# Attention and a feed-forward block in one kernel: strips of 64 key rows, two head pairs in one product

## The chip, the cores and the metric

The program runs on one core of a Trainium2 chip. Its time is the device time of one execution in microseconds (us). The core has five engines that run their own instruction streams and wait for each other by semaphores: TensorE (PE) for matrix products, VectorE (DVE), ScalarE (ACT), GpSimd (POOL) and SyncE (SP). Here POOL and SP do hardly any arithmetic: they issue DMA transfers. PE reads its operands from SBUF, an on-chip memory of 128 partitions, and writes into PSUM, which this kernel treats as eight banks of 128 partitions by 512 float32 columns.

## The reference

There are two stages. The first is attention with 4 batches, 8 heads, 768 positions and a head dimension of 64, where a query sees the 96 positions up to its own and the first 8 positions of the sequence (the global keys):

```python
scores = scale * np.matmul(q, k.transpose(0, 1, 3, 2))
rel = pos[:, None] - pos[None, :]
is_global = pos[None, :] < 8
is_local = (rel >= 0) & (rel < 96)
keep = is_global | is_local
dist = np.where(is_global & ~is_local, 96.0, np.abs(rel))
slopes = 2.0 ** (-(np.arange(8) + 1))
scores = scores - slopes[:, None, None] * dist
scores = np.where(keep, scores, -1e9)
a = np.exp(scores - scores.max(-1)); a = a / a.sum(-1)
x = np.matmul(a, v)
```

The eight heads side by side make 3,072 tokens of 512 numbers. The second stage is a gated feed-forward block (FFN) of width 1,536 over them:

```python
g = x @ w_gate
out = (g * (1 / (1 + np.exp(-g))) * (x @ w_val)) @ w_out
```

The output is float32, 3,072 by 512.

## The kernel before

**What sets the order.** The text `ORDER` (L39 to L118) lists some 1,500 steps, and the loop at its end (L726) runs them one after the other. Each step is a name with numbers, and each engine executes its own instructions in the order in which the steps stand. No scheduler moves anything. A step of DMA loads is issued by the engine that its function names: POOL for most loads (which convert float32 to float16 on the way), SP for the first ones, for transposing transfers and for the outputs, ACT for two early loads. A load that stands behind a step with a wait on the same engine waits too.

**Attention.** The 768 keys are cut into seven chunks of 120 rows (`KC`), and every chunk has the 8 global keys in front of it, so that a chunk fills the 128 partitions. Chunk c can only be seen by the 216 queries (`WIN`) from position 120c on. A step of scores (`c`, L471) multiplies the keys of some chunks with the queries that see them, for one pair of heads, into two PSUM banks. Batch 0 does this in four units per head pair (two of each half of 384 queries) with 128 key rows in a product; there a bias product (`B`, L461) first puts minus slope times distance into the banks, from `slopeI` (the identity times the slope) and `dist` (the table of distances). Batches 1 to 3 do it in two units per pair, with the chunk's lower and upper 64 rows in separate 64x64 products that leave out the queries that the 64 rows cannot see. `x` (L531) takes the exponential from PSUM into a buffer `at` in float16, up to three activations per unit, since the lower and upper rows cover different columns. Where no bias was added, `m` (L554) multiplies `at` with `masks`, the exponential of minus slope times distance, which ACT makes by `M` (L333) in two parts for each head.

**Sums and values.** `w` (L582) is issued three times per batch, group g of four heads and half: once with columns of ones for the sums of each query's weights, and twice with V, each time the even or the odd ones of its 64 columns, in four 32-wide tiles side by side. `i` (L612) turns the sums with a 32x32 block transpose and inverts them, `r` (L619) spreads the inverse back over the columns, `p` (L631) multiplies values by it and writes `xT`, the input of the FFN; `n` (L606) first copies the values out of PSUM, where the banks are wanted. One token block (a half of 384 queries of one batch) needs four such products, one for each pair of heads.

**FFN.** For each of 8 token blocks t and 12 column blocks f, `g` and `v` (L642) make gate and value products of 4 steps of 128x128 by 384 columns; the very first ones are cut in two (`ga` and `gb`), so that they can begin with half of `xT`. `t` (L653) takes a tanh on ACT, `s` (L657) and `h` (L664) finish the hidden block on DVE, `o` (L684) multiplies by w_out and `e` (L693) scales and stores. Weights come in slabs of 256 KB (`Lw`, L309), each needed before the first product that reads it.

**The start.** Batch 0 needs q and k turned by PE (`T`, L360: 6 transposes for one head pair, one half of the sequence, q or k). Its loads are 192 KB each: `Lf` on SP or ACT in float32 with a `cast` behind, `Lh` on POOL. Copies `k` and `q` (L368, L392) then bring the turned rows into `kT` and `qT`. `fill` (L339) is a run of products of ones that computes nothing. Batch 1 is turned by PE too (`U`), batches 2 and 3 by transposing transfers (`D`, L425). V comes in chunks of 120 rows (`Lv`, L264), `G` copies the 8 global rows in front of each chunk and `Z` clears the rows that no key has.

**PSUM.** `double` (L225) deals two neighbouring banks to scores and values, `single` (L235) one bank to everything else; a step that gets a bank waits on the chip until the bank's last reader is done.

## Time and profile before

Three runs took 237.44, 237.06 and 235.99 us; the median is 237.06. One further execution was recorded by the profiler; its own time is its span, 234.3 us from the first to the last instruction that the profile shows.

| Engine | busy, us | share of the span | instructions |
|---|---|---|---|
| PE (products) | 228.1 | 97% | 2,520 |
| PEld (weight loads, beside PE) | 132.0 | 56% | 2,520 |
| DVE | 171.5 | 73% | 422 |
| ACT | 134.6 | 57% | 240 |
| POOL | 77.3 | 33% | 103 |

The 16 DMA engines moved 25.5 MB in 88,196 packets; 68% of their time in the span went to the POOL queue's packets and 20% to those of SP and ACT. The mean rate over the span was 109 GB/s, and near 200 in the first third. The granted clock of PE is 9 tenths or more in all 40 slices of the page.

How to read the lines: a row names the line of the code, the engine, the operation, its output and inputs by the program's names (`banks` is PSUM), its shape in partitions by elements, the type, and a count. Groups give busy time and the mean of one in ns, then the time that the engine was idle just before, with what ended most of that idle time. The chain of waits gives start and length of each step in us.

### The profile page before, as it was taken

To read this page: it belongs to the slowest core of one execution; us is meant where nothing else is said; L and a number is where in the kernel's file an instruction comes from. 1 tells how busy PE (TensorE), PEld (TensorE's weight loads), DVE (VectorE), ACT (ScalarE), POOL (GpSimd) and SP (SyncE) were. 2 spreads that over 40 slices of the span, in tenths; PEclk is the share of its full clock that TensorE was granted. 3 is DMA by queue.
4 is the path that set the end of the run, shared out by engine and by line. 5 is a ranking of instruction groups with operands and counts; after the bars stand their busy time and mean duration, and the time that the engine had idled before them with its cause. 6 is when DMAs were issued, how large, how long until landed. Compare 5 with 4: busy or idle time off the path is not lost.

```text
span 234.3 us, 6170 instructions
## 1 busy us (share of the span) xinstructions
PE 228.1 (97%) x2520; PEld 132.0 (56%) x2520; DVE 171.5 (73%) x422; ACT 134.6 (57%) x240; POOL 77.3 (33%) x103
## 2 busy tenths in 40 slices
PE   6999999999999999999999999999999999999994
PEld 4466566555546655655555655555666556555442
DVE  3899998867888798889785788678858794835200
ACT  3899654797883624989834489963554143312031
POOL 8976485461999666880000000000000000000000
PEclk9999999999999999999999999999999999999999
DMA  6999999999999999999042261001110001000224
GB/s 177 173 182 205 197 194 200 192 156 201 141 134 186 158 183 158 181 158 151 3 134 60 83 111 45 22 26 45 48 48 0 4 0 45 4 0 0 90 109 159
DMA packets 88196, 25.54 MB, mean 109 GB/s; under 512 B 78016, under 2 KB 85224, under 8 KB 88168
## 3 DMA queue, kind: packets, MB, share of 16 engines
q0 software_dynamic: 66992, 13.77, 68.3%
q1 hardware_dynamic: 20488, 10.80, 20.4%
q10 hardware_dynamic: 688, 0.59, 0.7%
q8 instruction: 19, 0.31, 0.6%
q14 instruction: 9, 0.07, 0.1%
HBM read 28.51 MB, written 6.29 MB: 149 GB/s over the span
## 4 chain that ended last, share of the span: by engine, by line
PE 90%; DMA 4%; POOL 2%; DVE 1%; ACT 1%; issue 0%; DVEq 0%; POOLq 0%
PE banks L649 54%; PE banks L690 25%; PE banks L596 6%; PE banks L491 3%; DMA k<-in_k_dram 3%; DMA kN<-kst 1%; PE banks L679 1%; POOL vS L282 1%; POOL q L262 1%; PE banks L402 1%; PE banks L364 0%; POOL vS L267 0%; ACT kT L377 0%; POOL k L262 0%; DVE dT L615 0%
## 5 line engine op out<-in xcount | busy, mean ns | idle before, releaser
L655 ACT ACTIVATE th<-banks 128x384 f32<-128x384 f32 x96 | 44.5, 493 | 57.1 <-PE banks L649 55.7
L649 PE MATMUL banks<-xT,wv 128*128 128x384 f16 x384 | 73.5, 326 | 0.0
L649 PE MATMUL banks<-xT,wg 128*128 128x384 f16 x384 | 72.1, 326 | 0.0
L665 DVE TENSOR_TENSOR hT<-banks,sl 128x384 f16<-128x384 f32 x96 | 51.2, 550 | 23.2 <-PE banks L649 22.0
L690 PE MATMUL banks<-wo,hT 128*128 128x512 f16 x276 | 67.8, 379 | 0.0
L539 ACT ACTIVATE at<-banks 64x960 f16<-64x960 f32 (+6 forms) x76 | 58.7, 804 | 3.7 <-PE banks L491 2.5
L659 DVE SCALAR_TENSOR_TENSOR sl<-th,banks 128x384 f32<-128x384 f32 x96 | 50.7, 545 | 12.5 <-ACT th L655 11.9
L649 PEld LDWEIGHTS <-wv 128*128 128x128 f16 x384 | 36.6, 98 | 27.8 <-issue 0.3
L649 PEld LDWEIGHTS <-wg 128*128 128x128 f16 x384 | 36.9, 98 | 25.9
L690 PEld LDWEIGHTS <-hT 128*128 128x128 f16 x276 | 26.7, 98 | 27.1
L564 DVE TENSOR_TENSOR at<-at,masks 128x864 f16<-128x864 f16 (+5 forms) x62 | 25.5, 459 | 3.9 <-ACT at L539 3.9
L267 POOL DMA_DIRECT2D vS<-in_v_dram x28 | 25.4, 912 | 6.8 <-DMA qT<-qst 1.8
L708 ACT ACTIVATE osb<-banks 128x512 f32<-128x512 f32 x23 | 13.5, 597 | 24.2 <-PE banks L690 18.9
L305 POOL DMA_DIRECT2D kst<-in_k_dram x20 | 16.9, 846 | 11.4 <-PE banks L690 6.6
L305 POOL DMA_DIRECT2D qst<-in_q_dram x20 | 17.0, 860 | 3.6 <-DMA wo<-in_moe_w_out_dram 3.2
L491 PE MATMUL banks<-qT,kT 64*64 64x160 f16 (+9 forms) x408 | 12.3, 226 | 0.0
L596 PE MATMUL banks<-at,vS 128*32 128x216 f16 (+6 forms) x576 | 11.7, 225 | 0.1
L608 ACT COPY ns<-banks 128x768 f32<-128x768 f32 x10 | 7.9, 800 | 5.9 <-PE banks L596 5.9
L615 DVE STREAM_TRANSPOSE dT<-banks 128x384 f32<-128x384 f32 x16 | 9.2, 576 | 2.8 <-PE banks L596 2.5
L596 PEld LDWEIGHTS <-vS 128*32 128x32 f16 x576 | 9.8, 95 | 2.1 <-issue 1.9
L491 PEld LDWEIGHTS <-kT 64*64 64x64 f16 (+1 forms) x408 | 7.6, 104 | 5.6 <-issue 4.3
L632 DVE TENSOR_TENSOR xT<-ns,rb 128x384 f16<-128x384 f32 x20 | 10.5, 543 | 0.0
(57 smaller groups left out, 115.7 us busy)
## 6 DMA issues: line engine op xcount, KB each, us to landing
out_dram<-osb SPq DMA_DIRECT2D x23, 256.0 KB, 2.1
vS<-in_v_dram POOLq DMA_DIRECT2D x24, 120.0 KB, 7.0
qst<-in_q_dram POOLq DMA_DIRECT2D x20, 96.0 KB, 6.7
kst<-in_k_dram POOLq DMA_DIRECT2D x20, 96.0 KB, 6.1
wg<-in_moe_w_gate_dram POOLq DMA_DIRECT2D x6, 256.0 KB, 8.2
wv<-in_moe_w_val_dram POOLq DMA_DIRECT2D x6, 256.0 KB, 8.8
wo<-in_moe_w_out_dram POOLq DMA_DIRECT2D x3, 512.0 KB, 12.2
k<-in_k_dram POOLq DMA_DIRECT2D x3, 192.0 KB, 6.2
```

Of the source, the lines that this page charges most:

```text
L267: nc.gpsimd.dma_start(out=v_of(b)[r0:r0 + n, c, :, :], in_=v[b, :, KC * c:KC * c + n, :].rearrange("h p d -> p h d"))
L305: nc.gpsimd.dma_start(out=rows_of(i, b, h // 2)[:, :, h % 2, :], in_=KQ[i][b, h].rearrange("(t p) d -> p t d", p=128))
L491: nc.tensor.matmul(sc[k0:k1, hi, col:col + n], lhsT=keys[r, k0:k1], rhs=qTs[b, hp][r, q0:q0 + n], start=fresh, stop=True, skip_group_check ...
L539: nc.scalar.activation(out=out, in_=src, func=AF.Exp, scale=scale)
L564: ENG[e].tensor_mul(a2, a2, m[:, :, m0:m0 + n])
L596: nc.tensor.matmul(dst[r, o:o + n], lhsT=vSs[b][:, c, 4 * g + j, what - 1::2] if what else ones[:, 0:32], rhs=ats[b, hp, side(b, u)][:, j ...
L649: nc.tensor.matmul(gv[t, f, which][:, 0:TB], lhsT=w[:, c, 128 * f:128 * f + 128], rhs=xTs[t][:, c, :], start=(c == 0), stop=(c == NC - 1))
L655: nc.scalar.activation(out=th, in_=gv[t, f, 0][:, 0:TB], func=AF.Tanh, scale=0.5)
L659: nc.vector.scalar_tensor_tensor(out=sl, in0=gv[t, f, "t"], scalar=1.0, in1=gv[t, f, 0][:, 0:TB], op0=AluOp.add, op1=AluOp.mult)
L665: nc.vector.tensor_mul(hTs[t][:, f, :], gv[t, f, 1][:, 0:TB], gv[t, f, "s"])
L690: nc.tensor.matmul(ops_t[t, i], lhsT=hTs[t][:, f, 128 * i:128 * i + 128], rhs=wo[:, f, :], start=(f == 0), stop=(f == NFF - 1))
L708: nc.scalar.mul(out=osb, in_=ops, mul=0.5)
```

## The change

**Scores.** The 128 rows of a chunk are cut into a lower and an upper 64 rows for all batches, and a unit is now one strip: for one batch, one group g of four heads, one half of the queries, and lower or upper rows (`up`). Its 128 partitions hold the 64 rows for one head pair of the group and the same 64 rows for the other. Table `PIECES` says which chunk, which columns and which queries belong to a strip; strips are 480, 400, 488 and 504 columns wide for each of two heads. There are 32 strips in all, and each takes one exponential over all its columns and, in batches 1 to 3, one product with a mask. A buffer `at` is one of a rotating pool of eleven.

**Masks, distances.** The distance table has 64 rows for strips, held twice: the second copy is divided by 4, since the slope of the second pair of a group is a quarter of the first's. So four masks and four slopes serve eight heads, and a mask covers one half at a time (992 or 880 columns). The table comes in two loads.

**Values and sums.** A strip's rows for one pair stand on partitions 0 to 63 and for the other pair on 64 to 127, so the values use 64x64 tiles, four of them at once. Half of these tiles need V on the other 64 partitions than the one it was loaded to; `cross` (step `X`) copies those parts within SBUF by four SP transfers into `vX`. There are five such steps: two in batch 0, one in each later batch. The sums (`w`) are one step for all eight heads of a batch and half, with `pick` (ones in 16 columns for each pair) as the weights; `i` inverts them once for each batch and half, with two reciprocals and four copies of 32 rows; `r` spreads once for each of four `xT` rows.

**The rest.** The slabs of w_gate and w_val give each partition two rows of 1 KB at a distance of 128 rows instead of two neighbouring ones; V has two buffers instead of three; the clearing of corners of `at` (`zc`) is gone. `ORDER` is a new text with the new steps.

```diff
+PIECES = [
+    [[(1, 0, 120, 152), (0, 152, 0, 160), (2, 312, 240, 144), (3, 456, 360, 24)],
+     [(1, 0, 176, 160), (0, 160, 64, 152), (2, 312, 296, 88)]],
+    [[(3, 0, 384, 128), (4, 128, 480, 152), (5, 280, 600, 152), (6, 432, 720, 48),
+      (2, 480, 384, 8)],
+     [(3, 0, 416, 160), (4, 160, 536, 160), (5, 320, 656, 112), (2, 432, 384, 72)]],
+]
+WIDTH = [[480, 400], [488, 504]]
+COL0 = [[0, 480], [880, 1368]]
+COLS = 1872
...
+    return np.concatenate([d, d / 4]).astype(np.float16)
...
-Lf.S.0.1 zc.1.V Z.0.P pre Lf.A.1.1 cast.0.1.V Lf.A.1.0 Li sl.3 Ld.S Z.3.P fill.14 sl.7 sl.0 T.1.0.0
...
+Li pre Lh.0.0.4.8 Ld.S.1 fill.14 T.2.0.0 Lf.S.0.1 Lh.0.1.0.4 Z.0.P fill.2 Lh.1.0.4.8 Ld.S.0 sl.2
...
+    def cross(b, c0, c1):
+
+        if b not in crossed:
+            crossed[b] = sb2.tile([128, NCH, NP, D], FP16, name="vX", tag="vX")
+        for r in range(2):
+            to, of = slice(64 * r, 64 * r + 64), slice(64 - 64 * r, 128 - 64 * r)
+            for g in range(2):
+                h = 4 * g + 2 * r
+                nc.sync.dma_start(
+                    out=crossed[b][to, c0:c1, 2 * g:2 * g + 2], in_=vSs[b][of, c0:c1, h:h + 2])
...
-            in_=src[256 * g:256 * g + 256, f0:f0 + WF].rearrange("(p s) f -> p s f", s=2))
+            in_=src[256 * g:256 * g + 256, f0:f0 + WF].rearrange("(s p) f -> p s f", s=2))
...
+    def make_masks(i, half):
         nc.scalar.activation(
-            out=masks[:, h, c0:c1], in_=dist[:, c0:c1], func=AF.Exp, scale=-slopes[h])
-        made.add((h, part))
+            out=masks[:, i, columns(half)], in_=dist[:, columns(half)], func=AF.Exp,
+            scale=-slopes[4 * (i // 2) + i % 2])
+        made.add((i, half))
...
+    def bias(g, half, up):
+        w, x = WIDTH[half][up], COL0[half][up]
+        sc = scs[0, g, half, up] = double(("c", 0, g, half, up))
+        biased.add((0, g, half, up))
+        for hi in range(2):
+            nc.tensor.matmul(
+                sc[:, hi, 0:w], lhsT=slopeI[:, 2 * g + hi, :], rhs=dist[:, x:x + w],
+                start=True, stop=False, skip_group_check=True)
+
+    def scores(b, g, half, up):
...
+        for c, col, q0, n in PIECES[half][up]:
+            k0 = 128 * c + (0 if c else NG) + 64 * up
+            for r in range(2):
+                for hi in range(2):
+                    d = slice(64 * hi, 64 * hi + 64)
+                    nc.tensor.matmul(
+                        sc[64 * r:64 * r + 64, hi, col:col + n],
+                        lhsT=kTs[2 * g + r][d, k0:k0 + 64], rhs=qTs[b, 2 * g + r][d, q0:q0 + n],
+                        start=fresh, stop=True, skip_group_check=True)
+
+    def exps(b, g, half, up):
+        key, w = (b, g, half, up), WIDTH[half][up]
+        at = ats[key] = sb2.tile(
+            [128, 2, max(max(x) for x in WIDTH)], FP16, name="at", tag="at", bufs=11)
+        sc = scs.pop(key)
+        nc.scalar.activation(out=at[:, :, 0:w], in_=sc[:, :, 0:w], func=AF.Exp, scale=scale)
...
+    def mask(b, g, half, up, e):
...
+        a2 = ats[b, g, half, up][:, :, 0:w]
+        ENG[e].tensor_mul(a2, a2, masks[:, 2 * g:2 * g + 2, x:x + w])
...
+    def weigh(b, half, g):
+
+        num = nums[b, g, half] = double(("n", b, g, half))
+        todo = [(up, *p) for up in range(2) for p in PIECES[half][up]]
+        for x, (up, c, col, q0, n) in enumerate(todo):
...
+            for r in range(2):
+                k = slice(64 * r, 64 * r + 64)
+                for hi in range(2):
+                    h = 4 * g + 2 * r + hi
+                    nc.tensor.matmul(
+                        num[64 * hi:64 * hi + 64, r, q0 - HB * half:q0 - HB * half + n],
+                        lhsT=vSs[b][k, c, h] if up == r else crossed[b][k, c, 2 * g + hi],
+                        rhs=ats[b, g, half, up][k, hi, col:col + n],
+                        start=x == 0, stop=x == len(todo) - 1, skip_group_check=True)
+
+    def weigh_ones(b, half):
+
+        den = dens[b, half] = single(("d", b, half))
...
+                    den[32 * t:32 * t + 32, q0 - HB * half:q0 - HB * half + n], lhsT=pick,
+                    rhs=ats[b, g, half, up][:, hi, col:col + n],
...
+    def invert(b, half):
...
+        nc.vector.transpose(dT, dens[b, half][:, 0:TB])
+        release(("d", b, half))
+        src = dT.rearrange("p (n r i) -> p r n i", r=2, i=16)[:, :, :, 0]
+        for g in range(2):
+            nc.vector.reciprocal(out=dR[:, g], in_=src)
+        for g in range(2):
+            for t in (g, g + 2):
+                to = t + 1 - 2 * g
+                nc.vector.tensor_copy(out=dR[32 * to:32 * to + 32, g], in_=dR[32 * t:32 * t + 32, g])
```

Where the new text puts the steps is seen best on three engines. On **ACT**, from its first instruction on, before the change (a row is line, operation, output and input, shape, count; `masks<-dist` is a mask, `at<-banks` an exponential, `q<-in_q_dram` the issue of a load; numbers tell buffers apart):

```order
L258 DMA q_78<-in_q_dram 128x2x192 x2
L347 ACT_TABLE_LOAD
L347 CAST q_80<-q_78 128x384
L377 COPY kT_72<-banks 128x3x120
L377 COPY kT_72<-banks 128x24
L393 COPY qT<-banks 128x384
L335 ACTIVATE masks<-dist 128x432 x2
L539 ACTIVATE at_0_82<-banks 128x2x432
L335 ACTIVATE masks<-dist 128x432
L539 ACTIVATE at_0_82<-banks 128x2x168
```

The same place of the changed program:

```order
L347 ACTIVATE masks<-dist 128x992
L256 DMA q_79<-in_q_dram 128x2x192 x2
L347 ACTIVATE masks<-dist 128x992
L390 COPY kT_73<-banks 128x3x120
L390 COPY kT_73<-banks 128x24
L406 COPY qT<-banks 128x384
L390 COPY kT_72<-banks 128x96
L390 COPY kT_72<-banks 128x2x120
L390 COPY kT_72<-banks 128x48
L360 CAST q_81<-q_79 128x384
L347 ACTIVATE masks<-dist 128x992
L406 COPY qT<-banks 128x384
```

One mask now stands ahead of the two q loads and one behind them. Ahead of the first exponential stand three masks of 992 columns where there were two of 432; behind the last of these rows the first four exponentials follow each other.

**POOL**, from the last of six clearings of V's empty rows on, before (`vS` is V, `MEMSET vS` a clearing, the DMA rows are loads):

```order
L282 MEMSET vS 128x256
L262 DMA k_81<-in_k_dram 128x4x192
L262 DMA q_80<-in_q_dram 128x4x192 x2
L267 DMA vS<-in_v_dram 120x8x64
L262 DMA k_81<-in_k_dram 128x4x192
L262 DMA q_80<-in_q_dram 128x4x192
L262 DMA k_81<-in_k_dram 128x4x192
L267 DMA vS<-in_v_dram 120x8x64 x3
L312 DMA wg<-in_moe_w_gate_dram 128x2x512 x4
L312 DMA wv<-in_moe_w_val_dram 128x2x512 x2
```

After, where two loads of k (`k_82`) are POOL's first work and stand just ahead of these rows:

```order
L280 MEMSET vS 32x256
L280 MEMSET vS 128x256
L260 DMA q_81<-in_q_dram 128x4x192
L265 DMA vS<-in_v_dram 120x8x64 x3
L280 MEMSET vS 32x256
L280 MEMSET vS 128x256
L265 DMA vS<-in_v_dram 120x8x64
L260 DMA q_81<-in_q_dram 128x4x192 x2
L260 DMA k_82<-in_k_dram 128x4x192
L265 DMA vS<-in_v_dram 48x8x64
L303 DMA qst<-in_q_dram 128x4x384
L321 DMA wg<-in_moe_w_gate_dram 128x2x512 x2
```

No clearing stands ahead of the first loads any more, and the chunk of 48 rows of V and a load of batch 1's q (`qst`, 384 KB) have moved ahead of the first slab of weights.

**DVE**, from the first inverted sums on, which lead to the first `xT`, before (`dT` and `dR` are turned and inverted sums, `rb` the spread inverse):

```order
L615 STREAM_TRANSPOSE dT<-banks 128x384
L616 RECIPROCAL dR<-dT 128x12
L377 COPY kT_73<-banks 128x96
L377 COPY kT_73<-banks 128x2x120
L377 COPY kT_73<-banks 128x48
L615 STREAM_TRANSPOSE dT<-banks 128x384
L616 RECIPROCAL dR<-dT 128x12
L622 STREAM_TRANSPOSE rb<-dR 128x384 x2
L632 TENSOR_TENSOR xT<-banks,rb 128x384 x4
```

After:

```order
L544 STREAM_TRANSPOSE dT<-banks 128x384
L548 RECIPROCAL dR<-dT 128x24 x2
L552 COPY dR<-dR 32x24 x4
L390 COPY kT_74<-banks 128x96
L390 COPY kT_74<-banks 128x2x120
L390 COPY kT_74<-banks 128x48
L406 COPY qT<-banks 128x384
L556 STREAM_TRANSPOSE rb<-dR 128x384 x3
L566 TENSOR_TENSOR xT<-banks,rb 128x384 x3
L556 STREAM_TRANSPOSE rb<-dR 128x384
L566 TENSOR_TENSOR xT<-banks,rb 128x384
```

The sums of all eight heads are inverted together (one transpose, two reciprocals, four small copies), and four spreads instead of two lead to the four rows of `xT`.

408 lines of the change are left out of this document (137 added, 271 removed), and 3 rows, old and new, of the table SCORES.

## The prediction

> **What bounds the kernel now.** First I read busy time by stage (time in us and instruction count of each engine, then granted clock, mean share of the DMA engines, GB/s), because the page's 97% for PE is an average.
>
> ```profile
> core 0: us, PE busy (x) PEld busy (x) DVE busy (x) ACT busy (x) POOL busy (x), PEclk, DMA share, GB/s
> 5.20:18.60 13.40, 12.62 (x272) 8.36 (x271) 11.87 (x40) 11.85 (x29) 11.68 (x16) 1.00 1.65 177
> 18.60:34.00 15.40, 15.40 (x213) 9.31 (x212) 14.76 (x36) 11.34 (x27) 10.03 (x14) 1.00 1.39 198
> 34.00:60.00 26.00, 26.00 (x299) 15.23 (x301) 20.64 (x53) 17.72 (x30) 12.91 (x17) 1.00 1.66 183
> 60.00:110.00 50.00, 50.00 (x554) 28.59 (x543) 41.99 (x98) 34.19 (x55) 38.34 (x46) 1.00 2.02 166
> 110.00:170.00 60.00, 59.96 (x755) 34.58 (x753) 47.78 (x112) 39.06 (x63) 0.00 (x0) 1.00 0.21 57
> 170.00:231.00 61.00, 60.99 (x439) 33.93 (x437) 32.05 (x68) 18.62 (x37) 0.00 (x0) 1.00 0.10 36
> ```
>
> From 18.6 us to the end PE is never idle, and before that it loses only 0.8 of 13.4 us. Every other engine has slack. So PE's own work sets the end, and a change pays by what it takes from PE, less any hole it opens. The chain of waits gives the prices (start us, us, what, number of products):
>
> ```profile
> 18.66 0.76 PE banks L649 x4
> ...
> 32.02 1.64 PE banks L596 x100
> 33.66 4.66 PE banks L649 x28
> 38.32 1.46 PE banks L402 x48
> ...
> 45.65 0.76 PE banks L649 x4
> 46.41 0.65 PE banks L690 x3
> ...
> 49.65 0.65 PE banks L649 x4
> ...
> 230.32 0.68 PE banks L679 x12
> ```
>
> 28 products of 384 columns take 4.66 us: 0.433 ns per column. The 100 products at 32.02 are five sums of 696 columns, four 32-wide tiles side by side: 3,480 columns in 1.64 us, 0.44 ns after 0.1 us of entry. So packed tiles are paid by columns too. Four products behind a change of tile shape take 0.76 us, else 0.65: a change costs 0.11. The first FFN product stands at 18.6, the last at about 230.8: 212.2 us.
>
> **PE's saving.** Columns, four packed tiles counted once: scores 5,184 to 3,744 in batch 0 and 4,080 to 3,744 in batches 1 to 3; values 5,184 to 3,744 and sums 2,592 to 1,872 in each batch; bias 4,656 to 3,520. Together 53,184 to 40,960, so 12,224 x 0.433 = 5.3 us. Changes of tile shape along PE's order go from 80 to 67: 13 x 0.11 = 1.4. Pieces of 8, 24 and 48 columns must cost more than their columns, and no row shows them alone. Bounds: nothing, or the 16.4 ns per product of the row with 100 as a floor for each of 1,280 attention products, 21.0 us where columns give 16.2, which takes 4.8 of the 5.3 away. I take 0.2, since that row has 48-column pieces in it and still goes by columns. Saved: 6.5 us.
>
> The Trainium skill (TensorE: Matmul & The Clock Gate, section "Wait — 56ns, not 53.3ns?") says starts of products never come closer than about 25 ns, however small they are. By that rule about 1,280 small products cost 32 us before and after, and only the 1.4 us would be left of the saving. The 16.4 ns per product in the trace speaks against it for packed tiles.
>
> **ACT, DVE, queues later on.** The rows that price them (busy, mean ns of one, then idle before and what ended it):
>
> ```profile
> L539 ACT ACTIVATE at<-banks 64x960 f16<-64x960 f32 x24 | 23.2, 966 | 0.3
> L539 ACT ACTIVATE at<-banks 64x912 f16<-64x912 f32 x12 | 11.1, 921 | 0.8 <-PE banks L491 0.7
> L335 ACT ACTIVATE masks<-dist 128x432 f16<-128x432 f16 x8 | 4.5, 606 | 0.0
> L335 ACT ACTIVATE masks<-dist 128x216 f16<-128x216 f16 x8 | 2.6, 382 | 0.0
> L393 ACT COPY qT<-banks 128x384 f16<-128x384 f16 x4 | 1.9, 485 | 0.0
> L655 ACT ACTIVATE th<-banks 128x384 f32<-128x384 f32 x96 | 44.5, 493 | 57.1 <-PE banks L649 55.7 <-DVE sl L659 0.9
> L564 DVE TENSOR_TENSOR at<-at,masks 128x864 f16<-128x864 f16 x28 | 16.8, 601 | 3.9 <-ACT at L539 3.9
> L615 DVE STREAM_TRANSPOSE dT<-banks 128x384 f32<-128x384 f32 x16 | 9.2, 576 | 2.8 <-PE banks L596 2.5
> L616 DVE RECIPROCAL dR<-dT 128x12 f32<-128x12 f32 x16 | 3.7, 229 | 0.6
> L622 DVE STREAM_TRANSPOSE rb<-dR 128x384 f32<-128x384 f32 x16 | 9.0, 566 | 0.2
> L632 DVE TENSOR_TENSOR xT<-ns,rb 128x384 f16<-128x384 f32 x20 | 10.5, 543 | 0.0
> L377 DVE COPY kT<-banks 128x360 f16<-128x360 f16 (+4 forms) x12 | 3.1, 309 | 0.0
> ```
>
> The 32 exponentials of 800 to 1,008 elements at about 1 ns an element take some 30 us where 76 took 58.7 on the page; ACT wins over 20 us, but it already sits 55.7 us waiting for PE, so this is worth nothing by itself. DVE loses 34 mask products (about 7 us), gains 16 spreads (9 us), and its inversions stay near 13 us if one of the 32-row copies costs between 0.1 and 0.2; cover for it is its slack in every window. From about 35 us on I keep PE without holes, but allow 0.5 us for new waits.
>
> **The start is the other half.** There the kernel must reach its first FFN product, and each us PE idles is lost, since nothing later has slack. What stands on PE before that product in the new order: 16 transposes of 6 (0.18 each by the 48 in 1.46 us) 2.9, bias 1.5, all of batch 0's scores 1.6, sums and values of half 0 1.2, two whole transposes 0.7, twenty shape changes 2.1: near 9.8 us. The same sum over the old order gives 11.1. So of the 6.5 us saved 5.2 lie behind the first product, and from it on PE needs 212.2 - 5.2 = 207.0 us. The change breaks even if first product plus holes come to 230.8 - 207.0 = 23.8 us.
>
> DVE and ACT first. Issue and landing of the first loads:
>
> ```profile
> 0.73 1.04 ACTq L258 DMA_DIRECT2D q<-in_q_dram  x2
> ...
> q<-in_q_dram ACTq DMA_DIRECT2D x2, 192.0 KB, 3.3
> ...
> dist<-dist_c SPq DMA_DIRECT2D x1, 162.0 KB, 4.3
> ```
>
> Now ACT's first work is a mask of 992 columns (between the two L335 rows 1.04 ns a column, so 1.0 after the overlap of neighbours), and the two q loads are issued behind it. Distances land near 1.2 + 4.3 = 5.5; mask to 6.5; second q issue at 7.0, landing 4 us later (between 3.3 and 4.3) at 11.0; cast 0.4, mask 1.0, copy of q 0.4: 12.8. Four exponentials, 3.5 less overlaps: 16.1. The sum on PE and its handover 0.6: 16.7. DVE then inverts (0.576 + 2 x 0.229 + four copies, 1.5), copies k and q for the second half (1.1), spreads three (1.5), scales two (1.0): 21.8. Before, the masks of one head came to 432 columns and the q loads were ACT's first rows. PE puts two whole transposes and two shape changes (0.9) between: **22.6 us**. ACT's own chain (three copies, three exponentials, two masks behind the first four) frees the PSUM bank of that product at about 22, so cutting one chain alone does not help.
>
> Then the weights:
>
> ```profile
> 0.74 2.14 POOL L282 MEMSET vS<- 32x256 uint32 x6 [0.29 <-POOLq L745]
> 2.82 0.88 POOL L262 DMA_DIRECT2D k<-in_k_dram  x1
> ...
> 11.05 2.27 POOL L312 DMA_DIRECT2D wg<-in_moe_w_gate_dram  x3
> ...
> DMA to landing us min/median/max: 7.1/7.1/7.1
> ...
> vS<-in_v_dram POOLq DMA_DIRECT2D x6, 120.0 KB, 7.0
> k<-in_k_dram POOLq DMA_DIRECT2D x3, 192.0 KB, 6.2
> ...
> qst<-in_q_dram POOLq DMA_DIRECT2D x1, 384.0 KB, 8.7
> ```
>
> The first 256 KB slab is issued at 11.05 and lands 7.1 us later, 18.1. Ahead of it and with it went ten halves of q or k of 192 KB, four chunks of V of 120, identity 32 and distances 162: 2.85 MB. Now 384 KB of batch 1's q, a 48 KB chunk, 295 KB more of distances and 256 KB of V copied across also go first: 0.98 MB, 5.0 us more at 198 GB/s and 5.5 at 177. POOL starts its loads 2.1 us earlier, which is worth between nothing (DMA busy with the other queues) and 2.1. The slab lands between 21.0 and 23.6; at 22.3 it is no later than the 22.6 above. The next six slabs and two chunks of V follow at 1.3 and 0.7 us each. PE's order then wants the fourth slab after 2.3 us of products and the eighth piece after 3.2 more: waits of about 0.5 and 1.5, 2.0 us together (bounds 0.8 and 3.5), where the old order had other attention work to put in.
>
> **Sum.** 22.6 + 2.0 - 23.8 = +0.8, and 0.5 for new waits: **+1.3 us**. The saving of 6.5 is eaten by PE's idle start. On the profiled execution's 234.3 us this gives a span of 235.6; the 2.8 us between that span and the 237.06 us median stay, so 238.4 us.
>
> **Rivals.** (1) *Weights late*: the slab lands at 23.6 and the waits behind it are 3.5, since sixteen 64 KB copies across compete with it. 27.1 - 23.8 + 0.5 = +3.8: 240.9 us. For it: DMA share above 1.3 in both first windows; against: 7.1 us of landing time is partly queue. It decides from a slab at about 22.9. Chance 0.24.
> (2) *The start keeps its cover*: q lands at 10 and the chain loses nothing between steps, product at 20.0 and holes of 1.0: -2.8, 234.3 us. For it: PE lost only 0.8 us of that stage before. Against: every step of the chain is longer than its old one. Chance 0.20.
> (3) *Cold clock*:
>
> ```profile
> 2.11 3.17 PE L343 MATMUL banks<-ones 128*128 128x256 f16 x14 [2.11 <-DVE ones L323]
> ```
>
> Fourteen products of 256 columns take 0.226 us each, twice the later price per column: PE begins slow. Its filler now starts earlier and a hole follows before the first load, so the slow price may last. Then 9.8 us of work becomes up to 19.6 behind a first transpose at 6.3: 25.9 and holes of 0.6: +3.2, 240.3 us. Chance 0.12. The Trainium skill (same page, section "What's actually happening") puts the fall back to half rate at one idle window of about 3.4 us; no window of this run shows it, the granted clock is 1.00 in all.
> (4) *Fewer columns, same time*: the floor of 16.4 ns holds for every product, most of the 5.3 us is not saved: near 242.5. Chance 0.04.
>
> **How the numbers follow.** Forecast 0.40; it lies within 1% (2.4 us, about what a measurement of this kernel can tell from no change). Faster by over 1% is rival 2, 0.20; slower is rivals 1, 3 and 4, 0.40. The range reaches from rival 2 to past rival 1: 234.0 to 242.2; the likeliest case alone, with the bounds of slab and waits, spans 236.5 to 240.
>
> **What would show it.** Right: PE busy well under 10 of the first 13 us after its first transpose, the first FFN product at 21.5 to 23.5, PE idle 1 to 3 us before the eighth slab, no hole after 35 us, and about 207 us from the first FFN product to the last. Wrong: a first product before 21, a clock under 1.00 in the first 20 us, or holes at batches 1 to 3, where V copied across comes behind loads in the same queue.

## The result, and the profile after

The changed kernel takes **262.49 us** (median of 260.77 to 263.71), the kernel before 237.25 in the same comparison: a ratio of 1.109, 95% interval 1.103 to 1.115. The forecast was 238.4 us, within 234.0 to 242.2, with 0.4 on slower. The likeliest case was no change within 1%, at +1.3 us; it became +25 us, outside the range. Two executions of later runs are left out of their figures, one that ran at a granted clock of 0.665 and took 342.5 us, and one at 0.935 that took 263.8.

The profiled execution has a span of 259.0 us against 234.3. Busy time by stage, in the stretches used before (us and instruction count of each engine, then granted clock, DMA share, GB/s):

```profile
5.20:18.60 13.40, 8.06 (x108) 4.55 (x108) 5.33 (x17) 5.55 (x13) 10.86 (x17) 1.00 1.67 203
18.60:34.00 15.40, 10.00 (x252) 7.82 (x251) 10.63 (x28) 10.22 (x16) 9.06 (x13) 0.78 1.37 194
34.00:60.00 26.00, 25.80 (x302) 15.66 (x300) 24.20 (x56) 14.50 (x28) 17.85 (x23) 1.00 1.74 164
60.00:110.00 50.00, 40.54 (x476) 22.83 (x474) 35.54 (x84) 19.42 (x34) 28.33 (x35) 0.93 1.63 141
110.00:170.00 60.00, 57.84 (x715) 32.99 (x716) 48.01 (x113) 30.42 (x48) 6.92 (x8) 0.97 0.81 99
170.00:231.00 61.00, 60.97 (x517) 34.18 (x516) 39.35 (x87) 20.58 (x41) 0.00 (x0) 1.00 0.09 36
```

PE, which was idle for 0.8 us of the first of these stretches and for next to nothing behind it, now stands still for 5.3 of 13.4 us, 5.4 of 15.4, 9.5 of the 50 between 60 and 110, and 2.2 of the 60 behind that. What PE waited for (us in all, times, longest):

```profile
PE banks L480 <- DMA qT<-qst: 6.2, 2, 5.7
PE banks L514 <- DMA vX<-vS: 5.1, 1, 5.1
PE banks L377 <- DMA q<-in_q_dram: 3.3, 1, 3.3
PE banks L480 <- DVE kT L453: 3.3, 1, 3.3
PE banks L377 <- DMA k<-in_k_dram: 2.0, 1, 2.0
```

All five are transfers; the fourth is DVE's copy of transposed keys, which itself waited for its transfer. DVE executes in order, so work of the FFN that stands behind such a copy is late too: 1.4 us more, at 105 us, PE waits for a hidden block (`hT`) behind a copy of keys that DVE could begin only at 105.1, when its transfer had landed. The transposes of batch 1 that are transfers here are four, the queries and keys of head pairs 2 and 3; PE turns the other two pairs (`U`). The chain of waits (start, length, what) has the four transfers from issue to landing, and products behind the holes:

```profile
3.58 7.14 DMA q<-in_q_dram
...
19.49 7.60 DMA vX<-vS
...
52.49 14.65 DMA qT<-qst
...
68.22 3.71 PE banks L582 x12
...
72.50 2.06 PE banks L582 x12
...
100.60 10.37 DMA kN<-kst
...
113.41 2.66 PE banks L582 x8
```

A load of q on POOL's queue lands at 10.7 us, V copied across at 27.1, the last transpose of batch 1 at 67.1, a transpose of batch 2's keys at 111.0. Behind the hole that ends at 67.3, twelve FFN products take 3.71 us, and the next twelve 2.06.

**Where the 24.7 us are.** The first FFN product starts at 31.45 us instead of 18.60: +12.85. From it to the last product PE takes 224.1 us instead of 212.2. These two stretches, before and after, and three in which the granted clock is half:

```profile
18.59:230.78 212.19, 212.15 (x2238) 121.62 (x2236) 157.23 (x363) 120.73 (x211) 61.28 (x75) 1.00 0.87 102
```

```profile
31.45:255.55 224.10, 212.25 (x2159) 120.39 (x2159) 158.38 (x360) 94.14 (x166) 54.62 (x68) 0.98 0.84 95
...
23.80:30.60 6.80, 3.21 (x113) 3.16 (x115) 2.96 (x7) 2.00 (x3) 3.64 (x6) 0.50 1.53 189
64.70:71.50 6.80, 4.23 (x39) 2.46 (x40) 2.10 (x5) 2.19 (x3) 2.42 (x3) 0.50 1.67 158
...
112.50:115.90 3.40, 3.16 (x24) 1.49 (x22) 3.14 (x7) 1.80 (x2) 2.07 (x3) 0.50 1.65 194
```

PE is idle for 11.85 of the 224.1 us. In the two later stretches at half clock it is busy for 7.4 us; if each product takes about twice its time there, as in the rows of the chain, 3.7 us of that are lost (an estimate). That leaves 208.55 us of work, 3.65 less than before. 12.85 + 11.85 + 3.7 - 3.65 = 24.75.

What was forecast of ACT and of the start's DMA rows:

```profile
L490 ACT ACTIVATE at<-banks 128x1008 f16<-128x1008 f32 x8 | 8.1, 1009 | 3.1 <-PE banks L480 3.1
...
L556 DVE STREAM_TRANSPOSE rb<-dR 128x384 f32<-128x384 f32 x32 | 17.3, 562 | 0.1
...
L552 DVE COPY dR<-dR 32x24 f32<-32x24 f32 x32 | 7.1, 223 | 0.7
```

ACT's busy time fell from 134.6 to 110.3 us and bought nothing. DVE got the 16 more spreads that were forecast (17.3 us where there were 9.0), and a 32-row copy takes 0.223 us.

### The profile page after: what moved, and what is told of

It reads as the page before. It is cut to its first block, busy times and chain, and to the rows that moved or that the text cites. A ratio compares the mean times of both kernels' runs of the same rounds, so it can differ in the third digit from the quotient of the medians.

```text
span 259.0 us, 6134 instructions
## 1 busy us (share of the span) xinstructions
PE 231.2 (89%) x2516; PEld 133.2 (51%) x2516; DVE 173.5 (67%) x416; ACT 110.3 (43%) x192; POOL 77.1 (30%) x103
## 4 chain that ended last, share of the span: by engine, by line
PE 73%; DMA 15%; DVE 8%; issue 1%; POOL 1%; SPq 0%; DVEq 0%; POOLq 0%
PE banks L582 40%; PE banks L623 23%; DMA qT<-qst 6%; DMA kN<-kst 4%; PE banks L480 3%; DMA vX<-vS 3%; DMA q<-in_q_dram 3%; PE banks L514 3%; DVE xT L566 2%; PE banks L528 1%; PE banks L377 1%; DVE sl L592 1%; DVE hT L598 1%; PE banks L612 1%; DVE dR L552 1%
## 5 line engine op out<-in xcount | busy, mean ns | idle before, releaser
L582 PE MATMUL banks<-xT,wg 128*128 128x384 f16 x384 | 74.4, 330 | 1.7 <-DVE hT L598 1.4
L582 PE MATMUL banks<-xT,wv 128*128 128x384 f16 x384 | 75.5, 332 | 0.5 <-DVE sl L592 0.5
L598 DVE TENSOR_TENSOR hT<-banks,sl 128x384 f16<-128x384 f32 x96 | 51.2, 551 | 31.0 <-PE banks L582 30.6
L490 ACT ACTIVATE at<-banks 128x800 f16<-128x800 f32 (+3 forms) x32 | 29.1, 949 | 24.5 <-PE banks L480 24.2
L480 PE MATMUL banks<-qT,kT 64*64 64x160 f16 (+9 forms) x512 | 13.0, 236 | 10.6 <-DMA qT<-qst 6.2
L499 DVE TENSOR_TENSOR at<-at,masks 128x1008 f16<-128x1008 f16 (+3 forms) x28 | 17.2, 641 | 3.1 <-ACT at L490 3.1
L480 PEld LDWEIGHTS <-kT 64*64 64x64 f16 x512 | 10.2, 121 | 15.6 <-issue 10.1
L556 DVE STREAM_TRANSPOSE rb<-dR 128x384 f32<-128x384 f32 x32 | 17.3, 562 | 0.1
L566 DVE TENSOR_TENSOR xT<-ns,rb 128x384 f16<-128x384 f32 x28 | 14.7, 544 | 0.2
L514 PE MATMUL banks<-at,vX 64*64 64x160 f16 (+9 forms) x256 | 9.3, 223 | 5.1 <-DMA vX<-vS 5.1
L535 ACT COPY ns<-banks 128x768 f32<-128x768 f32 x14 | 10.6, 803 | 7.6 <-PE banks L514 7.5
L450 DVE COPY kT<-kN 128x720 f16<-128x720 f16 x10 | 4.9, 486 | 8.5 <-DMA kN<-kst 8.5
## 6 DMA issues: line engine op xcount, KB each, us to landing
wv<-in_moe_w_val_dram POOLq DMA_DIRECT2D x6, 256.0 KB, 10.5
wo<-in_moe_w_out_dram POOLq DMA_DIRECT2D x3, 512.0 KB, 12.8
```

The lines of the kernel that those rows point to most:

```text
L480: nc.tensor.matmul(sc[64 * r:64 * r + 64, hi, col:col + n], lhsT=kTs[2 * g + r][d, k0:k0 + 64], rhs=qTs[b, 2 * g + r][d, q0:q0 + n], start ...
L490: nc.scalar.activation(out=at[:, :, 0:w], in_=sc[:, :, 0:w], func=AF.Exp, scale=scale)
L499: ENG[e].tensor_mul(a2, a2, masks[:, 2 * g:2 * g + 2, x:x + w])
L556: nc.vector.transpose(rb.rearrange("p (n i) -> p n i", i=32), rbs[b, half][:, g, r].unsqueeze(2).broadcast_to([128, TB // 32, 32]))
L566: ENG[e].tensor_mul(x_of(2 * b + half)[:, 2 * g + r, :], nums[b, g, half][:, r, 0:TB], rbs[b, g, half, r])
L582: nc.tensor.matmul(gv[t, f, which][:, 0:TB], lhsT=w[:, c, 128 * f:128 * f + 128], rhs=xTs[t][:, c, :], start=(c == 0), stop=(c == NC - 1))
```

## The experiments

Times are medians of four executions (of ten for the light kernel before and for the copies behind), run beside the kernel before, which took 236.1 to 236.6 us in these comparisons and 237.25 in that of the changed kernel; the ratio is to that kernel, and 1.109 is that of the changed kernel. Unless it says otherwise, an edit is made to the changed kernel. "First FFN" is the start of the first FFN product in the profiled execution. Four executions of one kernel lie up to 3.7 us apart and a profile shows one of them, so two runs are told apart only where their intervals do not overlap.

| Run | us | ratio [95%] | first FFN | from there to the last product |
|---|---|---|---|---|
| changed kernel | 262.49 | 1.109 [1.103, 1.115] | 31.45 | 224.1 |
| batch 0 without copies across | 260.60 | 1.099 [1.091, 1.107] | 29.51 | 227.0 |
| w_out later | 257.01 | 1.088 [1.079, 1.096] | 32.11 | 219.6 |
| clearing later | 264.99 | 1.120 [1.113, 1.126] | 32.20 | 227.0 |
| no copies across | 259.91 | 1.096 [1.089, 1.103] | 30.13 | 225.4 |
| outputs on ACT's queue | 261.91 | 1.111 [1.105, 1.118] | 31.62 | 227.8 |
| q first | 262.22 | 1.111 [1.108, 1.114] | 31.95 | 225.3 |
| w_out and outputs | 257.08 | 1.090 [1.085, 1.094] | 32.33 | 219.7 |
| third kN buffer | 257.75 | 1.092 [1.086, 1.097] | 31.69 | 218.5 |
| globals early, q and k of batch 1 later | 262.80 | 1.111 [1.106, 1.117] | 29.85 | 228.7 |
| all moves | 257.39 | 1.090 [1.085, 1.096] | 30.88 | 223.3 |
| light changed kernel | 249.22 | 1.054 [1.048, 1.060] | 31.63 | 211.0 |
| light, w_out later | 250.78 | 1.061 [1.057, 1.065] | 33.01 | 212.7 |
| light, more filler | 248.77 | 1.047 [1.038, 1.056] | 32.04 | 213.1 |
| light kernel before | 237.60 | 1.005 [1.002, 1.007] | 19.88 | 212.7 |
| before, with copies across | 259.65 | 1.101 [1.095, 1.106] | 19.89 | 233.0 |
| before, copies behind | 238.73 | 1.009 [1.005, 1.012] | 18.59 | 213.7 |

### Which hole costs what

**Batch 0 without copies across.**

```diff
-                        lhsT=vSs[b][k, c, h] if up == r else crossed[b][k, c, 2 * g + hi],
+                        lhsT=vSs[b][k, c, h] if up == r or b == 0 else crossed[b][k, c, 2 * g + hi],
...
-... G.0.1.4.V G.0.4.7.S X.0.0.4 T.1.1.0 ... M.0.1 X.0.4.7 Lw.1.2.1 ...
+... G.0.1.4.V G.0.4.7.S T.1.1.0 ... M.0.1 Lw.1.2.1 ...
```

> Left out: in batch 0 nothing is copied across, and the half of its value tiles that would read the copy reads V where it lies (other rows of V, same shapes and number of products). Theory A (the holes are separate waits): the 5.3 us hole at 21.8 us goes with its slow products behind it, first FFN product at 25 to 26.5 us instead of 31.5, and the later holes stay as long as they are: time 6 to 7 us below the changed kernel, about 256. Theory B (transfers are behind by a fixed amount up to 67 us): the first FFN product comes early as in A, but the last transpose of batch 1 still lands at 65 to 67 us, so the hole that ends there grows from 5.9 to 10 us or more and the time falls by 0 to 3 us, about 260 to 262.

The first FFN product came only 1.95 us earlier, and the median fell by 1.9, with intervals that overlap. Theory A is out. Theory B is right about the time, but not in how: the hole before the last transpose of batch 1 did not grow. It was 3.8 us long instead of 5.7 and ended at 65.9 instead of 67.3. At the start the hole of 5.1 us was replaced by others:

```profile
26.10 0.72 PE L415 MATMUL banks<-ident,qst 128*64 128x128 f16 x19 [0.95 <-DVE xT L566]
29.09 0.48 PE L415 MATMUL banks<-ident,qst 128*64 128x128 f16 x5 [2.27 <-issue]
```

(start, length, then the idle time before and what ended it). DVE was only then done with the first rows of `xT`, and PE stood for 2.27 us for nothing that the profile shows. Behind these pauses the granted clock was half:

```profile
28.30:35.10 6.80, 6.01 (x23) 2.93 (x23) 2.74 (x5) 2.47 (x4) 4.01 (x6) 0.50 1.26 204
```

The first sixteen FFN products took 5.1 us, where they take 2.6 in the changed kernel, so nothing of the earlier start was left behind them.

**No copies across at all.**

```diff
-                        lhsT=vSs[b][k, c, h] if up == r else crossed[b][k, c, 2 * g + hi],
+                        lhsT=vSs[b][k, c, h],
```

with all steps `X` taken out of the order.

> Left out: V is copied across in no batch; the half of the value tiles that would read the copy reads V where it lies (other rows of V, same products). It prices all twenty transfers. Theory A: as without those of batch 0 alone (6 to 7 us), and 1 to 2 us more since four of them run beside the transposes of batch 1: 8 us below the changed kernel, about 254. Theory B: 2 to 4 us below, about 259.

2.6 us below: twenty transfers of 1.8 MB are not by themselves what makes the kernel slow, although PE waits 5.1 us for the first of them.

**w_out later.**

```diff
-c.1.0.0.0 Lo.0 X.1.0.7 h.1.1 c.1.0.1.1 h.1.9 Lo.1 Lo.2 Lr.2.0.1 ... Lr.2.0.2 h.1.8
+c.1.0.0.0 X.1.0.7 h.1.1 c.1.0.1.1 h.1.9 Lr.2.0.1 ... Lr.2.0.2 Lo.0 Lo.1 Lo.2 h.1.8
```

> Only the three loads of w_out (512 KB each) move on POOL, behind seven loads of batch 2, so that they are issued some 6 us later. If the transposes of batch 1 are late because these 1.5 MB share the DMA engines with them, the last one lands at 60 to 63 us instead of 67.1, and the hole before it shrinks from 5.9 to 1 to 3 us: time 3 to 5 us below the changed kernel. If they are late because their own rows arrive late and transposes follow each other in one queue, nothing moves: within 1 us.

5.5 us below, the largest single gain. What PE waited for in this run:

```profile
PE banks L511 <- DMA vX<-vS: 8.3, 3, 5.6
...
PE banks L477 <- DMA qT<-qst: 1.1, 2, 0.7
```

The wait for transposes fell from 6.2 to 1.1 us. The last one of batch 1 landed at 62.8 us, 10.6 after issue instead of 14.65. So it was late because 1.5 MB of w_out shared the DMA engines with it. The other profiles agree: where the w_out loads are issued at 48.5 to 51.6 us, that transpose takes 14.3 to 16.3 us (eight runs); where they are issued ahead of 46 us or from 56.9 on, it takes 9.0 to 10.6 (six). 2.7 us came back as two waits for V of batch 1 copied across, which now had the w_out loads beside it.

**Clearing later.**

```diff
-... D.2.2.1 g.3.6 Z.3.P g.3.0 Lr.3.0.2 ... K.3.2 Lv.3.4 ...
+... D.2.2.1 g.3.6 g.3.0 Lr.3.0.2 ... K.3.2 Z.3.P Lv.3.4 ...
```

> Only the clearing of V's third use of a buffer (batch 3, POOL waits 8.2 us there for the last values of batch 1, since V has two buffers now) moves behind POOL's loads of batch 2 and most of batch 3. Theory A: loads go on from 79 us, the transposes of batch 2 land about 3 us after issue where they took 9 to 10, and the holes of 1.6, 0.6 and 3.5 us between 104 and 112 shrink to 0 to 2 together: 3 to 6 us below the changed kernel. Theory B (what these transposes wait for is their place in SP's queue behind outputs and DVE): within 1 us.

2.5 us slower, with intervals that overlap: the expected gain of theory A did not come, and with loads running on from 79 us the transposes of batch 2 still took 8.5 to 10.5 us to land. The pause of POOL had not been the cause.

**Outputs of block 0 on ACT's queue.**

```diff
-            nc.sync.dma_start(out=out[r0:r0 + 128, :], in_=osb)
+            (nc.scalar if t == 0 else nc.sync).dma_start(out=out[r0:r0 + 128, :], in_=osb)
```

> One word: the three outputs of the first token block are issued by ACT instead of SP, so that SP's transposes of batch 2 no longer stand behind them (SP sat 22 us there, until 86.4). Theory C (place in SP's queue): the first transpose of batch 2 is issued at 76 to 80 us instead of 87.4, the last that PE waits for lands before 105, and the holes of 1.6, 0.6 and 3.5 us between 104 and 112 go to under 2 together with the slow products behind them: 4 to 7 us below the changed kernel, about 257. Theory D (the later ones wait for DVE to free the two kN buffers, or they share the DMA engines with V and the rows of batch 3): only the first ones come earlier, the holes lose under 2 us, time 260 to 262.

Theory D: 261.9 us. SP's transposes of batch 2 in this run:

```profile
77.48 2.61 SPq L443 DMA_TRANSPOSE kN<-kst  x2
85.99 2.60 SPq L443 DMA_TRANSPOSE qT<-qst  x2
...
103.51 2.19 SPq L443 DMA_TRANSPOSE kN<-kst  x1
```

The first came 10 us earlier, but the one that PE waits for was issued at 103.5, where the changed kernel has 100.6, and PE's waits there were 0.9 and 4.1 us. This profile is of the slowest of the four executions (264.59 us), with a hole of 8.8 us at batch 1 instead of 5.7, so that all behind it stands some 3 us later; the move gained nothing at its own place.

**w_out and outputs, and a third buffer for transposed keys.** The two edits above together, and in the second run this one with them:

```diff
-            dst = kNs[b, hp] = sb2.tile([128, S], FP16, name="kN", tag="kN", bufs=2)
+            dst = kNs[b, hp] = sb2.tile([128, S], FP16, name="kN", tag="kN", bufs=3)
```

> Both the w_out loads behind seven loads of batch 2 and the outputs of block 0 on ACT's queue. If the two holes are separate, the savings add: what the w_out run saved (5.5 us) plus what the run with the outputs alone saves, 250 to 253. If the holes pass time on to each other, it is no better than the better of the two alone by more than 1 us.

> The run with w_out late and outputs of block 0 on ACT, plus a third buffer for transposed keys (kN). If the transposes of batch 2 wait for DVE to free two buffers (the third one was issued at 95 to 100 us, 10 us behind the second), the third is issued at 88 to 92 us now, ahead of the burst of V and rows of batch 3, and the last one that PE waits for lands 2 to 5 us earlier: the holes between 102 and 109 (4.3 us) shrink to under 2, time 253 to 255. If sharing with that burst alone makes them late, they stay: 256 to 258.

257.1 and 257.8 us: neither adds to what w_out alone gave. With three buffers the third keys were issued at 91 us as expected, but the fourth landed at 105.9, and the holes there stayed (4.8 us together, where the changed kernel has 5.4).

### The start

**q first.**

```diff
-Li pre Lh.0.0.4.8 Ld.S.1 fill.14 T.2.0.0 Lf.S.0.1 Lh.0.1.0.4 Z.0.P fill.2 Lh.1.0.4.8 Ld.S.0 sl.2
-sl.3 sl.0 cast.0.1.V M.1.1 Lf.A.1.0 T.2.0.1 Lf.A.1.1 k.2.0.V Lv.0.0 M.2.1 Lf.S.0.0 T.0.1.0 T.1.0.0
+Li pre Lh.0.0.4.8 Ld.S.1 fill.14 T.2.0.0 Lf.S.0.1 Lh.1.0.4.8 Lh.0.1.0.4 Z.0.P fill.2 Ld.S.0 sl.2 sl.3
+sl.0 cast.0.1.V Lf.A.1.0 Lf.A.1.1 M.1.1 T.2.0.1 k.2.0.V Lv.0.0 M.2.1 Lf.S.0.0 T.1.0.0 ...
```

and `T.0.1.0 k.0.1.A` behind `T.1.0.1`.

> Only the start: the two q loads of ACT are issued ahead of its first mask, POOL's first load of q stands second instead of third, and the k transposes that need the load which thereby comes later move behind the first q transposes of all pairs. Theory: PE's first q transposes start near 8.5 us instead of 10.8, the first exponential near 14.5 instead of 16.5, and the first FFN product 1 to 2.5 us earlier (29 to 30.5), limited then by V copied across. Of the time 0 to 2 us is saved if the transposes of batch 1 still land at 66 to 67 (the later hole grows by what the start saves); 2 to 3 us if holes are separate.

The first q transposes started at 10.0 instead of 10.76, not at 8.5: k, issued first as before, now landed 2 us later (PE waited 4.1 us for it, where it had waited 2.0). V across landed at 27.1 as ever, the first FFN product came at 31.95.

**Globals early; batch 1's q and k later.**

```diff
-... cast.0.0.V T.0.0.0 q.1.0.A k.0.0.V ... T.1.1.1 G.0.1.4.V G.0.4.7.S X.0.0.4
+... cast.0.0.V T.0.0.0 q.1.0.A G.0.1.4.V k.0.0.V ... T.1.1.1 G.0.4.7.S X.0.0.4
```

and, in the second run, `L4.1.0 L4.0.0` ahead of `Lr.1.1.6`, with the steps `U.1.1 qw.1.A U.0.1 qw.0.A` ahead of `U.0.0`.

> Only DVE's copy of the global rows of V in batch 0 moves ahead of one copy of keys that waits for PE. The two transfers of V across that read these rows are issued at 16.5 to 17 us instead of 18.9 and 19.5, and land at 24.5 to 25.5 instead of 27.1; the first FFN product follows 1.5 to 2.5 us earlier, at 29 to 30. Of the time 0 to 1 us is saved, since the transposes of batch 1 land when they did.

> The same, and the two 384 KB loads of batch 1 move behind the weight slabs, with the PE transposes that use them. If V copied across lands late because it shares the DMA engines with these loads and slabs, it lands at 22 to 24 us, the slabs 2 to 3 us earlier than in the changed kernel (18.5 to 20 for the first), and the first FFN product at 26 to 28.5. If its 7 us are its own, it lands at 24.5 to 25.5 as with the globals alone. The time falls by 0 to 2 us in either case, as the transposes of batch 1 still wait for rows and w_out.

The globals alone gave 260.5 us [ratio 1.096 to 1.110], no gain that can be told. In the second run V across was issued at 15.8 to 18.3 us and landed at 25.0 and 25.7 at the end, 7.4 to 7.8 us after issue as in the changed kernel (7.3 to 8.4). So the 384 KB loads alone do not make its time to land. By the expectation that would leave a time of its own, but larger transfers of the same kind land within 2.3 to 4.0 us once POOL's loads are over (the run with copies behind, below); which load makes it long at the start stays open. The first FFN product came at 29.85, 1.6 us earlier, and the time did not fall.

**Three moves, and all moves.** The first has w_out later, the outputs on ACT's queue and q first; the second has w_out later, the outputs, the third buffer, the globals early and batch 1's q and k later.

> The start of the q-first run, w_out late and outputs of block 0 on ACT together. With the hole at 61 us gone (it was 0.9 us in the w_out run), what the start saves is kept only as far as the transposes of batch 1 land earlier too: 1 to 2.5 us below the run with the two moves if they do, no gain if that hole opens again by the same amount. Time 248 to 253.

> All moves together: globals early, batch 1's loads behind the slabs, w_out late, outputs of block 0 on ACT, three kN buffers. If the holes are late transfers and nothing else, what each run saved at its place adds where the next transfer is not the bound: 2 to 4 us below the run with the third kN buffer, 249 to 252, still over 5 per cent above the kernel before.

256.8 us (256.5 to 260.0) and 257.4 us: no better than w_out alone. With all moves, V across was issued earlier still and took longer:

```profile
L288 SPq DMA_DIRECT2D vX<-vS x4: 590/637/675, 15.5 to 17.6; - x4
...
DMA to landing us min/median/max: 8.2/8.9/9.1
```

Its last transfer was issued 1.9 us earlier than in the changed kernel and landed 0.6 us earlier. The Trainium skill (DMA: Bandwidth & Descriptors, section "Queues, rings and completion order") says that each DMA engine serves the queues in turn, a packet from each. No run tests the turns themselves. What they show is in keeping with it: in the run with copies behind, SP's transfers of 112 KB take 7.7 to 9.0 us at 73 us beside POOL's loads, and 2.3 to 4.0 behind 135 us, where POOL loads nothing.

### Transfers or queues

**Light kernels.** V of batches 1 to 3 is left out of both kernels, which takes transfers away and no work from PE. It also empties their places in the queues of POOL and SP, so the pair tells how much hangs on these transfers, and not whether by their bytes or by their places.

```diff
     def v_of(b):
+        b = 0
```

The same line stands in `cross` and where V is read, so that the values of all four batches are made with V of batch 0. Out of the order go the steps of batches 1 to 3 that load V (`Lv`), copy its global rows to the other chunks (`G`), clear its buffer (`Z`) and, in the changed kernel, copy it across (`X`).

> Left out of the changed kernel: V of batches 1 to 3 is neither loaded, cleared nor copied across; their values use V of batch 0 (same products). That takes 2.4 MB of V as it lands, and 1.3 MB copied across, off the DMA engines between 37 and 130 us, and nothing off PE. If the holes behind 60 us come from sharing the DMA engines, both shrink: 67.1 becomes 62 to 64, the transposes of batch 2 land in 5 to 7 us instead of 10, time 251 to 256. If they come from the order of queues and from buffers, it stays at 260 to 263.

> Left out of the kernel before: the same, V of batches 1 to 3 is not loaded, their values use V of batch 0. It has no holes that lighter traffic could close: 235 to 237.5, within 0.5 per cent of the kernel before. If it too were held by its transfers here and there, it would fall by more than 1 us.

The changed kernel falls to 249.2 us, by 13 us; the kernel before does not gain (ratio 1.002 to 1.007). The longest of PE's waits in the light changed kernel, and its transposes' median time to land (last number):

```profile
PE banks L510 <- DMA vX<-vS: 5.3, 1, 5.3
...
PE banks L476 <- DVE sl L588: 1.8, 1, 1.8
...
PE banks L476 <- DMA qT<-qst: 0.7, 1, 0.7
```

```profile
qT<-qst SPq DMA_TRANSPOSE x10, 4.0
kN<-kst SPq DMA_TRANSPOSE x10, 3.6
```

Those medians were 7.0 and 8.2 us in the changed kernel. They fell at batches 2 and 3; the four transposes of batch 1 still took 9.5 to 12.0 us. The 1.8 us that the second row puts down to DVE are PE's wait for the last of them, which landed at 63.2 us, 0.1 before PE went on. From the first FFN product to the last:

```profile
31.63:242.66 211.03, 208.24 (x2159) 118.88 (x2159) 156.41 (x360) 94.03 (x166) 34.85 (x43) 1.00 0.62 82
```

That is 208.2 us of work at full clock, and holes of 1.8 and 0.7 us. All that the light form still loses to the kernel before is at the start.

**Light, w_out later.** The edit of the w_out run on the light form.

> Left out as in the light form of the changed kernel, and the w_out loads behind seven loads of batch 2 besides. If sharing the DMA engines makes all holes behind 60 us, hardly one is left: first FFN product at 31.5, 207 to 210 us of work behind it and 3.4 us at the end, a span of 242 to 245 and a time of 244 to 248; what remains over the kernel before is the start. If queues and buffers make them, 255 to 258.

250.8 us, no gain over the light form. There the w_out loads were issued at 42.9 to 44.4 us, ahead of the transposes of batch 1; this edit puts them at 48.8 to 50.2, beside the last one, which took 14.3 us to land again. So it missed its 244 to 248 by a start that was 1.4 us later and by 3.3 us of waits for transposes (2.3 of them for that one).

**Light, more filler.** `fill.14` and `fill.2` become `fill.24` and `fill.20`.

> The light form of the changed kernel (V of batches 1 to 3 left out) with 24 and 20 filler products instead of 14 and 2, so that PE hardly stands still before the first q lands. If the slow price of products between 10.8 and 16 us comes from PE's standing still before, the 24 transposes and first bias products run at half that price, the first exponential comes 1 to 2.5 us earlier than 16.5 and the first FFN product at 29.5 to 31, limited by V copied across; time 0 to 2 us below the light form. If the slow price stays for another reason, nothing moves, or the filler stands in the way by up to 2 us.

The first two bias products took 0.51 us instead of 0.85, so their price was that of a PE that had stood still. But PE's first q came 1.9 us later in this run, at 12.6; the first exponential started at 16.55 as before, V across landed at 27.2, and the first FFN product came at 32.0: no gain that can be told.

**The kernel before with copies across.** `cross` is added to it with a buffer that nothing reads; first each copy stands where its V is complete, then those of batches 1 to 3 stand behind transposes.

```diff
-... G.1.1.7.S ... Lv.1.4 ... D.2.0.0 ...
+... G.1.1.7.S ... Lv.1.4 X.1.0.7 ... D.2.0.0 ...
```

```diff
-... Lv.1.4 X.1.0.7 ... D.1.3.1 ... D.2.0.0 ...
+... Lv.1.4 ... D.1.3.1 ... D.2.0.0 X.1.0.7 ...
```

> The kernel before with the twenty transfers that copy V across added on SP at the places where its V is complete, with nothing that reads the copies. If V copied across is dear by its traffic alone (64 KB to 112 KB in short runs beside all other loads), transposes and loads of the kernel before come late too and it takes 2 us or more longer, 239 to 242. If it is dear only where values wait for it and where the order asks for transposes early, the kernel before stays within 1 us: 235.5 to 238.

> Again the kernel before with the twenty transfers that copy V across and no reader, but those of batches 1 to 3 stand behind the transposes of their own batch in SP's queue, where V has already landed. The run before lost 15.9 us in one hole at 66 us, behind transfers that waited in SP's queue for V ahead of the last transpose of batch 1. If that place made the whole loss, the time is back within 2 us of the kernel before, 236 to 238.5, and the copies' traffic costs next to nothing in the old order. If their traffic makes the transposes late, it stays over 243.

The first takes 259.65 us. PE's longest wait, and SP's for V ahead of its copies (us, times, longest):

```profile
PE banks L499 <- DMA qT<-qst: 15.7, 1, 15.7
```

```profile
SPq L290 <- DMA vS<-in_v_dram: 39.2, 3, 13.2
```

SP stood for V with one transpose of batch 1 behind it. The second form takes 238.73 us, 0.9% over the kernel before [0.5 to 1.2%]: the same twenty transfers, all issued by 147 us, cost 2 us once nothing that PE needs soon is queued behind them. In that run the copies at the start took longer to land than in the changed kernel, and nothing waited:

```profile
vX<-vS SPq DMA_DIRECT2D x4, 64.0 KB, 9.6
```

### What the orders ask for

The DMA engines are about as loaded in the old order (share 1.66 from 34 to 60 us, 1.74 in the new). The orders differ in how much work PE has done when it first reads a transposing transfer of batch 1. PE's FFN and output products before that point, in the kernel before (59.7 us) and in the changed one (61.2 us), busy us and count first:

```profile
0.00:59.70 59.70, 31.05 (x176) 16.49 (x176) 1.00 1.49 186
0.00:59.70 59.70, 6.16 (x24) 2.35 (x24) 1.00 1.49 186
```

```profile
0.00:61.20 61.20, 26.87 (x159) 15.30 (x160) 0.94 1.53 178
0.00:61.20 61.20, 0.00 (x0) 0.00 (x0) 0.94 1.53 178
```

37.2 us of products cover the loads in the old order, 26.9 in the new. The three transposes of batch 1 whose landing the old trace has came at 56.2 to 61.5 us; the new order asked 10.3 us of work sooner and got the last one at 67.1. By the clock both orders read at nearly the same time, 59.7 and 61.5 us, because the new start is 12.85 us late, and the new order even issues its transposes earlier (47.0 to 52.5 us against 50.1 to 56.9). What lies beside them differs: the old order issued w_out at 31.0 to 33.7 us and had it by 47.2, the new one issued it at 49.7 to 51.2 and had it at 66.6. That the place of w_out made the hole at batch 1 is shown by the w_out run. No run moved FFN work ahead of these reads, so that such an order would close the holes is argued, not shown.

## Why the prediction was wrong

**What bounds the kernel before: right.** PE does. Less traffic gains it nothing, and 1.8 MB more of it costs 0.9% where nothing waits behind them.

**PE's saving: right in the main.** 6.5 us were forecast, 5.2 of them behind the first FFN product, and so 207.0 us from there to the last. The light form, at full clock, has PE busy for 208.2 us, the changed kernel 208.55 by the estimate above: about 4 of the 5.2 us came. Rival 4, which left 1.7 us of the whole saving, is out; which term gave less was not measured.

**"From about 35 us on I keep PE without holes, but allow 0.5 us for new waits": wrong, the largest step.** Holes of 11.85 us and some 3.7 us of slow products stand there. The step looked at each engine's slack in the old kernel, where DMA was about as full as in the new one, and took the transposes as given. Their landing times were in the old trace (median 4.5 to 6.2 us, up to 8.9), and so was the point of PE's work at which the old order reads them. The new order reads them earlier in PE's work and issues the w_out loads beside them instead of ahead of them. That count was never made. The part of the loss that hangs on this step is shown: with w_out elsewhere 5.5 us go, and with V of batches 1 to 3 left out all that was lost behind the start goes (211.0 us from the first FFN product to the last, against 212.2 before).

**The start: "22.6 us" was 31.45.** Two terms failed. V copied across was counted as 256 KB of traffic ahead of the weights, and not as a transfer that the first values wait for: 7.6 us from issue to landing, and its issue waits for V and for DVE. And the first exponential started at 16.5, not 12.8. The sum reached 12.8 by ACT's two loads of q alone. But PE's first q is POOL's third load, which landed at 10.7, and all but one of PE's first transposes stand behind it in its order: PE was busy for 5.74 of the 5.80 us from 10.7 to 16.5, at up to 1.7 times the later price (two bias products in 0.85 us, later 0.51). The sum had PE's 9.8 us of work there (its terms add up to 10.0) beside the chain and not in it. Rival 2 had q nearly right, at 10, and the product at 20.0 behind it. Neither term alone is the bound: without the copies the first product came at 29.5, with q moved up at 31.95. No run removed both, so how the 8.85 us over the forecast divide between them stays open.

**The weights: right.** The first slab, forecast at 22.3, landed at 21.95, and PE's waits for slabs are 0.3 us where 2.0 were allowed. Rival 1 had the right sign and the wrong transfer; of its sixteen copies of 64 KB batch 0 has eight, four of 64 KB and four of 48.

**Rival 3, the slow clock: there, but not as the bound.** Products behind holes cost about twice as much for a while (12 in 3.71 us, then 12 in 2.06), some 3.7 us behind 60 us, and about 1.6 more in the 3.2 us that PE is busy at half clock just ahead of the first FFN product (an estimate from the rows above). So a hole costs more than its length, and in the run without copies in batch 0 this took back what the earlier start had won. The sign that rival 3 was to show, a clock under 1.00 in the first 20 us, is not in the changed kernel's rows, which read 1.00 there although the products are dear; the profile of the run with the third kN buffer, where they cost the same, reads 0.50 from 7.5 to 14.3 us. The Trainium skill (TensorE: Matmul & The Clock Gate, section "What's actually happening") puts the way back to full rate at about 3.4 us of work. Here 4.2 us pass from the product at 67.27 to the end of the half clock at 71.5, after a wait of 5.7 us, which agrees roughly. More filler took 40% off the price of the first bias products and moved the end by nothing.

**ACT and DVE: right.** 24 us less on ACT and 8 us more spreads on DVE hardly show in the end: PE waits 0.5 us once, at 78.6, for DVE behind its inversion.

## What to carry to other kernels

A change of order moves the reads of transfers against the work that hides them. Before counting a saving, note for every transfer that the engine reads how much of the engine's work stands ahead of that read in the old and in the new order, and hold it against the landing times in the old trace under load. The twenty transfers added to the old order cost 0.9% at a good place in the queue and 10% at a bad one: ask what stands behind a transfer in its queue, and who waits for it. With the DMA engines full, most moves here only shifted the wait to another transfer; what helped was to take a large load away from beside a transfer that PE waits for (5.5 us), and fewer transfers (13 us). More work ahead of the read should help too, but no run tried it.
